# A dense layer's last chunk goes from tiles of 384 tokens to seven products per 2x2 blocks, and expert weight forms are made earlier

## The chip, the cores and the metric

One core of one Trainium2 chip runs the kernel. The metric is device time in microseconds (us) of one execution. Engines: PE (TensorE, matmuls), DVE (VectorE), ACT (ScalarE), SP (SyncE, here only the queue that issues DMAs). PSUM banks hold what TensorE accumulates; VectorE or ScalarE reads it out, here called an eviction.

## The reference

Three layers follow each other on 2304 tokens of width 512: an attention through 32 packed rows per head, a dense layer, and eight experts under a normalised routing matrix. The change touches the dense layer and when the first weights of the experts are prepared.

```python
def _moe_ref(x, w_in, w_out):
    h = x @ w_in                              # 2304x512 @ 512x2048
    g = h * (1.0 / (1.0 + np.exp(-h)))        # silu
    return (g @ w_out).astype(np.float32)     # 2304x2048 @ 2048x512
...
    for e in range(E):                        # 8 experts, after a gate P
        h = np.maximum(x @ w1[e], 0.0)
        out += P[:, e:e + 1] * (h @ w2[e])
```

## The kernel before

Every float32 operand of a product is kept as a rounded high part and a low rest ("hi", "lo"), and each product is three matmuls, hi x hi, hi x lo and lo x hi. Making such a pair is called a split: ScalarE casts the raw tile to hi, then VectorE subtracts hi from the raw tile and writes lo (`split`, L144 to L146). So each split is one ScalarE and one VectorE instruction, and VectorE waits for ScalarE's part.

The dense layer runs in four chunks of 512 hidden columns (`WID`, numbers 0 to 3). In chunks 1 to 3 the loop goes over the four batches of 576 tokens, in chunk 3 in the order 2, 3, 0, 1, and over two halves of 288 tokens each:

- `make_u` (L629) folds the chunk's first weights into the 128 packed attention rows; its 16 matmuls come once per batch and are split into `Uh`, `Ul`.
- `gemm1` (L675) makes the hidden values of a half: 24 matmuls of 288 columns (L652), then per pair of column tiles a silu into `graw` (ScalarE), a cast into `ring` (ScalarE) and the rest into `ring` (VectorE, L685).
- `gemm2_wide` (L723) takes the second matrix for 384 tokens and 128 output columns: 12 matmuls of 384 columns (L736) on a PSUM tile `g2w`. The result is added to the running sum `x2` (tiles `x2a` for batches 0 and 1, `x2b` for 2 and 3), on every other tile by VectorE (L743), on the rest by ScalarE, which puts the sum into PSUM ahead of the matmuls (L721) and copies it out (L741). A chunk has 24 such tiles.

Work for later runs in between. A generator `pre_w1` prepares, for 16 expert weight halves (numbers s = 0 to 15), four sums on VectorE (`sums4`, tiles `S`, L851) and four splits into tiles `po`, which SP stores to DRAM (L841); the raw weights of half s+1 are loaded (`r`, L823) when the sums of half s have been read. Each half takes seven steps of the generator, of which 111 are left when chunk 1 begins. `pump`, called after each pair of column tiles and each wide tile, advances it by `RATE[c]` steps per unit; a chunk has 64 units. Another generator, `convs`, turns the next chunk's 64-bit weights into floats and, for the second matrix, splits them into `woh`, `wol` (L544, L546). In chunk 3 its place is taken by `pre0`, which splits the tokens (`xs`) and the first expert weights (`w1h`, `w1l`, `w2h`, `w2l`) for the stage that follows; that stage begins on TensorE with the gate's matmuls (`lg`, L1235).

The order on TensorE, VectorE and ScalarE is the order in which the code is written. Each engine runs its queue in that order, so an instruction that waits holds up all behind it. PSUM tiles for `g2w` come from a pool of four (`ps3`), those for `gemm1` and `make_u` from a pool of two (`pg`).

Of the kernel before, what the change touches and what calls it, by code (L numbers as in the profile page):

```python
# [9 lines left out]
F32 = mybir.dt.float32  # L10
F32R = mybir.dt.float32r
# [3 lines left out]
ALU = mybir.AluOpType  # L15
# [10 lines left out]
FH = 512  # L26
EPS = 1e-9

RATE = {1: 36 / 64, 2: 36 / 64, 3: 41 / 53}
CONV = 0.6  # L30
TW = 384
LATE = 3
# [73 lines left out]
def fused_kernel(  # L106
# [34 lines left out]
    def unit(shape, dt, name):  # L141
        return wp.tile(shape, dt, tag="w", name=name)
# [98 lines left out]
    win, wout = {}, {}  # L241
# [306 lines left out]

    def convs(c):

        todo = [conv2(c, kind, j) for kind in ("in", "out") for j in range(2)]
        for g in todo[:2]:
            next(g)
        for _ in range(4):
            yield
        for n, g in enumerate(todo):
            for _ in g:
                yield
            if n + 2 < 4:
                next(todo[n + 2])  # L560
            yield
# [797 lines left out]

    with tc.manual_schedule(engines={mybir.EngineType.PE, mybir.EngineType.DVE, mybir.EngineType.Activation}):  # L1360
        for i, (c, b) in enumerate(seq):
            if c == 0:
                continue
            nxt = seq[i + 1] if i + 1 < len(seq) else None

            def pump(w):
                if cvn is not None:
                    if c < NC - 1:
                        pump_conv(w)
                    elif w > 1:  # L1370
                        cvn.step()
                pump_pre(w * RATE[c])

            if b == order[c][0]:
                cvn = Rot([convs(c + 1)], 1) if c + 1 < NC else None
            for half in range(2):
                unit_ = 2 * (b % 2) + half
                if c == NC - 1 and b == order[c][0] and half == 0:
                    cv_st.close()
                if c == NC - 1 and b == order[c][2] and half == 0:  # L1380
                    a2b_st.close()
                    open_("gh", 6)
                    open_("r2", 2)
                    load_w2(0, 0)
                    load_w2(0, 1)
# [4 lines left out]
                if half == 1 and nxt is not None and not first:  # L1390
# [6 lines left out]
                if (c, b) == seq[NC][:2]:  # L1397
                    keep = len(tiles)
                if nxt is None and half == 1:
                    keep = 0  # L1400
                while len(tiles) > keep:
                    n = tiles.pop(0)
                    gemm2_wide(*n, tiles[0] if tiles else None, pump)
                    if n == (NC - 1, order[c][2] // 2, 0, 3):
                        for _ in pre:
                            pass
                        cvn = Rot([pre0()], 1)
        cvn.drain()


    def moe_step(s):
# [150 lines left out]
```

## Time and profile before

| what | value |
|---|---|
| median of 3 runs (lowest, highest) | 1787.64 us (1787.37, 1788.65) |
| profiled execution, its span from first to last instruction | 1785.8 us |
| its own time | not listed beside the span; the median lies 1.84 us above the span |
| TensorE, VectorE, ScalarE busy | 1765.9, 1438.8, 1067.5 us |
| chunk 3, from its first `make_u` to the first `lg` | 279.6 to 373.05 us, 93.45 us |

Times in the rows are us from the span's start. Busy time is a sum of recorded durations; the records of two neighbours on an engine overlap by up to a tenth of a us, so what an instruction really takes in a queue is read from start to start.

### The profile page before, as it was taken

How to read it: one execution, taken by the hardware profiler on the slowest of the kernel's cores; microseconds unless marked ns; L12 is line 12 of the kernel's file. 1: busy time of each engine (PE TensorE's matmuls, PEld its weight loads, DVE VectorE, ACT ScalarE, POOL GpSimd, SP SyncE). 2: the span in 40 equal slices, each digit the busy share in tenths (PEclk: the TensorE clock that was granted, in tenths of full speed). 3: DMA queues.
4: the chain of work that ended last, by engine and by line, in shares of the span. 5: the costliest groups of instructions: out<-in, count | busy, mean ns of one | idle time of the engine just before them, and what ended most of it. 6: DMA issues, size and time to landing. Idle time of an engine off the chain costs nothing.

```text
span 1785.8 us, 25355 instructions
## 1 busy us (share of the span) xinstructions
PE 1765.9 (99%) x9564; PEld 1506.5 (84%) x9564; DVE 1438.8 (81%) x1917; ACT 1067.5 (60%) x1696; POOL 1.0 (0%) x8
## 2 busy tenths in 40 slices
PE   7999999999999999999999999999999999999998
PEld 4999999989998888888888888888888888888887
DVE  7868796758676998999888999887777777777778
ACT  6776676645454666665666665656555555555555
POOL 0000000000000000000000000000000000000000
PEclk9999999999999999999999999999999999999999
DMA  9326676965665655455655545964455544555442
GB/s 348 143 95 214 235 260 246 335 253 180 210 209 172 224 184 177 167 191 192 195 171 175 172 175 199 323 228 165 153 171 161 164 153 144 167 161 168 151 130 94
DMA packets 141498, 341.75 MB, mean 191 GB/s; under 512 B 11952, under 2 KB 49472, under 8 KB 140480
## 3 DMA queue, kind: packets, MB, share of 16 engines
q1 hardware_dynamic: 141376, 340.14, 56.3%
q8 instruction: 75, 1.23, 0.3%
q14 instruction: 47, 0.39, 0.1%
HBM read 256.66 MB, written 83.44 MB: 190 GB/s over the span
## 4 chain that ended last, share of the span: by engine, by line
PE 94%; DVE 2%; DMA 2%; ACT 1%; issue 1%; SPq 0%; DVEq 0%; ACTq 0%
PE d L1153 34%; PE X L1201 19%; PE Z L1201 10%; PE g2w L736 8%; PE g L652 5%; PE Y L1201 5%; PE u L1046 5%; PE d L1065 4%; PE g L704 3%; DMA v<-in_v_dram 1%; PE u L251 1%; DMA kq<-in_kT_dram 0%; PE pp L367 0%; PE s L251 0%; PE lg L1235 0%
## 5 line engine op out<-in xcount | busy, mean ns | idle before, releaser
L146 DVE TENSOR_TENSOR lo<-hb,hi 128x1024 fp32r<-128x1024 f32 x224 | 273.7, 1222 | 33.2 <-ACT hi L145 32.3
L1153 PE MATMUL d<-hi,w2f 128*128 128x512 f32 x896 | 294.2, 389 | 0.0
L1201 PE MATMUL X<-xf,w1l 128*128 128x512 f32 x1152 | 276.9, 389 | 0.0
L145 ACT CAST hi<-hb 128x1024 fp32r<-128x1024 f32 x224 | 235.3, 1052 | 65.2 <-PE d L1153 59.9
L1201 PEld LDWEIGHTS X<-xf,w1l 128*128 128x128 f32 x1152 | 216.2, 188 | 44.9
L1161 ACT COPY M<-d 128x512 f32<-128x512 f32 x234 | 137.3, 588 | 143.2 <-PE d L1153 140.1
L1165 DVE TENSOR_TENSOR M<-d,M 128x512 f32<-128x512 f32 x204 | 140.5, 689 | 101.2 <-PE d L1153 101.2
L1153 PEld LDWEIGHTS d<-hi,w2f 128*128 128x128 f32 x896 | 168.1, 188 | 35.0
L1153 PE MATMUL d<-lo,w2f 128*128 128x512 f32 x448 | 174.3, 389 | 0.0
L1153 PE MATMUL d<-hi,w2l 128*128 128x512 f32 x512 | 167.7, 389 | 0.0
L736 PE MATMUL g2w<-ring,woh 128*128 128x384 f32 x576 | 148.0, 337 | 1.9 <-ACT g2w L721 1.9
L1149 ACT COPY d<-M 128x512 f32<-128x512 f32 x216 | 127.1, 589 | 20.4 <-DVE M L1165 19.0
L1153 PE MATMUL d<-hi,w2g 128*128 128x512 f32 x384 | 125.7, 389 | 0.0
L1153 PEld LDWEIGHTS d<-hi,w2l 128*128 128x128 f32 x512 | 96.1, 188 | 20.3 <-ACT d L1149 0.4
L736 PEld LDWEIGHTS g2w<-ring,woh 128*128 128x128 f32 x576 | 102.7, 188 | 11.6 <-issue 7.5
L1208 ACT COPY cp<-X 128x512 f32<-128x512 f32 x128 | 74.4, 581 | 47.8 <-PE X L1201 47.6
L1153 PE MATMUL d<-lo,w2l 128*128 128x512 f32 x256 | 99.6, 389 | 0.0
L1153 PEld LDWEIGHTS d<-lo,w2f 128*128 128x128 f32 x448 | 84.1, 188 | 17.4
L1201 PE MATMUL Y<-xf,w1f 128*128 128x512 f32 x384 | 97.3, 389 | 0.0
L736 PE MATMUL g2w<-ring,wol 128*128 128x384 f32 x288 | 96.4, 335 | 0.0
L1046 PE MATMUL u<-xs,w1h 128*128 128x256 f32 x512 | 94.4, 285 | 0.0
L145 ACT CAST w1f<-rb 128x512 fp32r<-128x512 f32 x96 | 59.8, 624 | 56.9 <-PE d L1153 41.4
(219 smaller groups left out, 3474.5 us busy)
## 6 DMA issues: line engine op xcount, KB each, us to landing
r<-in_moe_w_dram SPq DMA_DIRECT2D x128, 512.0 KB, 4.1
w1l<-w1d SPq DMA_DIRECT2D x128, 512.0 KB, 4.2
w1d<-po SPq DMA_DIRECT2D x64, 512.0 KB, 4.5
w2d<-w2f SPq DMA_DIRECT2D x64, 512.0 KB, 4.2
w2l<-w2d SPq DMA_DIRECT2D x64, 512.0 KB, 3.6
rb<-in_moe_w_dram SPq DMA_DIRECT2D x96, 256.0 KB, 2.7
sb<-in_moe_w_dram SPq DMA_DIRECT2D x48, 256.0 KB, 2.7
pb<-pd SPq DMA_DIRECT2D x16, 512.0 KB, 5.3
```

What stands on the lines that cost most here:

```text
L145: act.copy(out=hi, in_=raw)
L146: eng.tensor_tensor(out=lo, in0=raw, in1=hi.bitcast(F32), op=ALU.subtract)
L652: pe.matmul(ps, lhs[:, fs], rhs, start=(n == 0), stop=(n == 5))
L736: pe.matmul(ps[:, :TW], lhs[:, f % 2, ds], ring[f // 2][:, 2 * (f % 2) + rhs, q], start=(n == 0 and not on), stop=(n == 11), skip_group_ch ...
L1046: pe.matmul(ps[:, i], w[:, k % 2, f], x[:, k], start=(n == 0), stop=(n == 11))
L1065: pe.matmul(ps, h[:, l, f % 2, 128 * tt:128 * tt + 128], w[:, f % 2], start=(fh == 0 and n == 0), stop=(fh == 1 and n == 11))
L1149: act.copy(out=ps, in_=m)
L1153: pe.matmul(ps, w[:, l, c, 128 * d:128 * d + 128], r[:, c], start=(n == 0 and not seed), stop=(n == 5), skip_group_check=seed)
L1161: act.copy(out=m, in_=ps)
L1165: dve.tensor_tensor(m, ps, m, op=ALU.add)
L1201: pe.matmul(ps, w[:, l, c, 128 * i:128 * i + 128], x[:, r, c], start=(n == 0 and p in (1, 7)), stop=(n == 5), skip_group_check=p in (2, 6, ...
L1208: act.copy(out=t, in_=ps)
```

## The change

Chunks 1 and 2 keep their loop. Their `RATE` goes from 36/64 to 41/64 steps per unit. At the end of chunk 2, `conv2` no longer splits chunk 3's second matrix but leaves the raw floats in `wz`. Chunk 3 is written out by hand. `w_forms` makes seven weight forms `wS` out of the 2x2 blocks of the second matrix. `g_unit` makes hidden values, raw, for one half and two column tiles; `h_form`, `forms_a`, `forms_b`, `forms_c` make the seven token forms `ft` of a batch out of four raw blocks. `product` takes one of seven products with 2 x 6 matmuls of 288 columns on PSUM tiles `sX`, `sZ` or `sY`, all from the pool of four. Four products go into `sX` one after another (1, 6, 5, 3), two into `sZ` (7, 4); after each the state of the PSUM tile is added to an output block by VectorE, and the next product adds on top of it in the same PSUM tile. Product 2 starts from the running sum, put into `sY` by ScalarE. `step` advances `pre_w1` by 0.9 per product or wide tile; after product 2 of the third batch the rest of it is run through at once.

```diff
-RATE = {1: 36 / 64, 2: 36 / 64, 3: 41 / 53}
+RATE = {1: 41 / 64, 2: 41 / 64, 3: 0.9}
...
+            if c == NC - 1:
+                wz[j] = z.rearrange("p (k f) -> p k f", k=2)
+                return
...
+        def step():
+            pump_pre(RATE[c])
+            next(cvn, None)
...
+            form(1, a11)
+            yield
+            dve.tensor_tensor(tb, a11, a21, op=ALU.subtract)
+            form(7, tb)
+            yield
+            dve.tensor_tensor(ta, a21, a22, op=ALU.add)
+            form(5, ta)
...
+        def h_form(k, p, x):
...
+            t = box["ft"][:, fn[0] % 4].rearrange("p (l c s) -> p l c s", l=2, c=2)
+            fn[0] += 1
+            split(t[:, 0], t[:, 1], x)
+            box["f"][k, p] = t
...
+        def forms_b(k):
+            r = box["raw"][k]
+            minus(r[12], r[22], r[12])
+            h_form(k, 7, r[12])
+            minus(r[5], r[22], r[11])
...
+        CH = {1: "X", 6: "X", 5: "X", 3: "X", 7: "Z", 4: "Z", 2: "Y"}
...
+        def product(k, p):
+            w, t, ch = wS[p], box["f"].pop((k, p)), CH[p]
+            for d in range(2):
+                if p in (1, 7):
+                    box[ch, d] = box["p3"].tile([128, 512], F32, tag="y", name=f"s{ch}{k}{d}")
+                ps = box[ch, d][:, :HS]
...
+                if p == 2:
+                    act.copy(out=dst, in_=ps)
+                else:
+                    dve.tensor_tensor(dst, ps, dst, op=ALU.add)
+            step()
...
+        for k in range(4):
...
+            product(k, 1)
+            if more:
+                g_unit(k + 1, 0, 0)
+            h_form(k, 5, r[11])
+            product(k, 7)
+            h_form(k, 2, r[21])
+            product(k, 6)
+            if more:
+                g_unit(k + 1, 0, 1)
+            h_form(k, 3, r[22])
+            product(k, 4)
...
+            product(k, 5)
+            if more:
+                forms_b(k + 1)
+                g_unit(k + 1, 1, 0)
+            product(k, 2)
+            if k == 2:
+                for _ in pre:
+                    pass
+                cvn = pre0()
+            if more:
+                forms_c(k + 1)
+            if k < 2:
+                make_u(c, o[k + 2])
+            product(k, 3)
+            if more:
+                h_form(k + 1, 4, box["raw"][k + 1][5])
```

Three places show how instructions move. The first is VectorE at the head of chunk 3, before: from the first `make_u` of the chunk (`Ul_3387`) on, VectorE has wide tiles' evictions, rests of `ring`, and expert forms.

```order
L638 TENSOR_TENSOR Ul_3387<-u_3377,Uh_3386 128x1024
L743 TENSOR_TENSOR x2b_1372<-g2w_3403,x2b_1372 128x384
L146 TENSOR_TENSOR po_6_3419<-S_2_3333,po_6_3419 128x512
L146 TENSOR_TENSOR po_7_3424<-S_3_3352,po_7_3424 128x512
L685 TENSOR_TENSOR ring_103<-graw,ring_103 128x2x288
L685 TENSOR_TENSOR ring_1745<-graw,ring_1745 128x2x288
```

The same place now, the last 12 of the 34 rows from `Ul_3416` to the eviction of the first product (`sX_3654`); `wsa` is the scratch of `w_forms`, `raw` a raw hidden block, and among the 22 rows ahead of these stand five `wS`, eight expert rows and three evictions.

```order
L641 TENSOR_TENSOR Ul_3621<-u_3611,Uh_3620 128x1024
L1460 TENSOR_TENSOR raw_3468<-raw_3470,raw_3468 128x576
L146 TENSOR_TENSOR ft<-raw_3468,ft 128x576
L1460 TENSOR_TENSOR raw_3471<-raw_3470,raw_3467 128x576
L1427 TENSOR_TENSOR wsa<-ct_3045,wsa 128x512
L146 TENSOR_TENSOR wS_3629<-wsa,wS_3629 128x512
L146 TENSOR_TENSOR ft<-raw_3471,ft 128x576
L1460 TENSOR_TENSOR raw_3471<-raw_3469,raw_3471 128x576
L146 TENSOR_TENSOR wS_3649<-ct_3045,wS_3649 128x512
L146 TENSOR_TENSOR ft<-raw_3471,ft 128x576
L1509 TENSOR_TENSOR x2b_1369<-sX_3654,x2b_1369 128x288
L1509 TENSOR_TENSOR x2b_1370<-sX_3662,x2b_1370 128x288
```

All weight forms and the first four token forms now stand in VectorE's queue ahead of the first product's eviction.

The second place is VectorE near the end of chunk 3, before: the expert forms of the last half (s = 15: `S_1_4149` to `po_3_4205`) stand around a wide tile's eviction, and the tokens' splits (`xs`) follow.

```order
L851 TENSOR_TENSOR S_4_4168<-r_151_4048,S_2_4151 128x512
L743 TENSOR_TENSOR x2a_790<-g2w_4174,x2a_790 128x384
L146 TENSOR_TENSOR po_6_4190<-S_2_4151,po_6_4190 128x512
L146 TENSOR_TENSOR po_7_4195<-S_3_4166,po_7_4195 128x512
L146 TENSOR_TENSOR po_5_4200<-S_1_4149,po_5_4200 128x512
L146 TENSOR_TENSOR po_3_4205<-S_4_4168,po_3_4205 128x512
L146 TENSOR_TENSOR xs_4224<-x2b_1369,xs_4223 128x128
```

Now, after product 2 of the third batch: eight rows of half 14 (`S_1_4295` to `po_3_4322`, not shown) and these of half 15 stand in one piece, ahead of a token form, a subtraction, and the eviction of the third batch's product 3 (`sX_4114`, `sX_4122`).

```order
L854 TENSOR_TENSOR S_1_4327<-r_150_4303,r_151_4305 128x512
L854 TENSOR_TENSOR S_2_4329<-S_1_4327,r_150_4303 128x512
L854 TENSOR_TENSOR S_3_4331<-r_150_4303 128x512
L854 TENSOR_TENSOR S_4_4333<-r_151_4305,S_2_4329 128x512
L146 TENSOR_TENSOR po_6_4339<-S_2_4329,po_6_4339 128x512
L146 TENSOR_TENSOR po_7_4344<-S_3_4331,po_7_4344 128x512
L146 TENSOR_TENSOR po_5_4349<-S_1_4327,po_5_4349 128x512
L146 TENSOR_TENSOR po_3_4354<-S_4_4333,po_3_4354 128x512
L146 TENSOR_TENSOR ft<-rawt,ft 128x576
L1460 TENSOR_TENSOR rawt<-rawt 128x576
L1509 TENSOR_TENSOR x2a_787<-sX_4114,x2a_787 128x288
L1509 TENSOR_TENSOR x2a_788<-sX_4122,x2a_788 128x288
```

Sixteen expert rows that were spread over the chunk, with evictions between them, now follow one another.

The third place is TensorE beside it, now: products 2 and 3 of the third batch (`sY_4240`, `sX_4114`), then 1, 7 and 6 of the fourth (`sX_4384`, `sZ_4406`, `sX_4384` again). Before, wide tiles stood here.

```order
L1501 MATMUL sY_4240<-ft,wS_3649 128x288 x6
L1501 MATMUL sY_4242<-ft,wS_3649 128x288 x6
L1501 MATMUL sX_4114<-ft,wS_3629 128x288 x6
L1501 MATMUL sX_4122<-ft,wS_3629 128x288 x6
L1501 MATMUL sX_4384<-ft,wS_3488 128x288 x6
L1501 MATMUL sX_4392<-ft,wS_3488 128x288 x6
L1501 MATMUL sZ_4406<-ft,wS_3509 128x288 x6
L1501 MATMUL sZ_4414<-ft,wS_3509 128x288 x6
L1501 MATMUL sX_4384<-ft,wS_3568 128x288 x6
L1501 MATMUL sX_4392<-ft,wS_3568 128x288 x6
```

In the fourth batch no hidden values are left to make, so the products follow each other with nothing between them.

## Rows read from the trace of the kernel before

**Rows 1.** The page, busy time of each engine.

```profile
PE 1765.9 (99%) x9564; PEld 1506.5 (84%) x9564; DVE 1438.8 (81%) x1917; ACT 1067.5 (60%) x1696; POOL 1.0 (0%) x8
```

**Rows 2.** Waits, those of PE: waited for, us in total, times, longest.

```profile
PE g2w L736 <- ACT g2w L721: 1.9, 2, 1.6
```

**Rows 3.** Windows: stretch, PE, PEld, DVE, ACT, POOL busy, PEclk, DMA share, GB/s.

```profile
10.00:15.00 5.00, 4.47 (x37) 2.06 (x38) 3.53 (x7) 1.86 (x4) 0.00 (x0) 1.00 1.02 418
...
133.00:213.00 80.00, 78.20 (x526) 74.64 (x525) 64.00 (x92) 53.23 (x84) 0.00 (x0) 1.00 0.70 243
213.00:279.60 66.60, 66.28 (x443) 62.55 (x441) 54.73 (x78) 46.58 (x75) 0.00 (x0) 1.00 0.62 230
...
279.60:373.05 93.45, 93.45 (x617) 88.71 (x616) 63.41 (x101) 58.51 (x107) 0.00 (x0) 1.00 0.77 282
```

**Rows 4.** Timeline of PE: start, duration, instructions, idle before and releaser.

```profile
179.21 0.62 PE L736 MATMUL g2w<-ring,woh 128*128 128x384 f32 x2 [1.63 <-ACT g2w L721]
...
284.91 0.29 PE L652 MATMUL g<-a2h,Uh 128*128 128x288 f32 x1
...
288.10 0.51 PE L736 MATMUL g2w<-ring,woh 128*128 128x384 f32 x2
...
292.26 0.29 PE L652 MATMUL g<-a2h,Uh 128*128 128x288 f32 x1
...
295.54 1.09 PE L251 MATMUL u<-win,ppT 64*32 64x512 f32 x16
296.56 0.62 PE L736 MATMUL g2w<-ring,woh 128*128 128x384 f32 x2
...
373.05 2.17 PE L1235 MATMUL lg<-x2b,wg 128*32 128x256 f32 x26
```

**Rows 5.** Timeline of DVE in chunk 3.

```profile
282.04 1.22 DVE L638 TENSOR_TENSOR Ul<-u,Uh 128x1024 fp32r<-128x1024 f32 x1
...
350.38 0.76 DVE L685 TENSOR_TENSOR ring<-graw,ring 128x576 fp32r<-128x576 f32 x1 [0.85 <-ACT ring L684]
351.06 0.69 DVE L851 TENSOR_TENSOR S<-r,r 128x512 f32<-128x512 f32 x1
351.78 0.69 DVE L851 TENSOR_TENSOR S<-S,r 128x512 f32<-128x512 f32 x1
...
353.59 0.55 DVE L743 TENSOR_TENSOR x2a<-g2w,x2a 128x384 f32<-128x384 f32 x1
354.06 2.49 DVE L146 TENSOR_TENSOR po<-S,po 128x512 fp32r<-128x512 f32 x4
356.46 0.29 DVE L146 TENSOR_TENSOR xs<-x2b,xs 128x128 fp32r<-128x128 f32 x1
356.66 0.29 DVE L146 TENSOR_TENSOR xs<-x2a,xs 128x128 fp32r<-128x128 f32 x1
...
374.20 1.22 DVE L146 TENSOR_TENSOR w2l<-r,w2h 128x1024 fp32r<-128x1024 f32 x1
375.33 0.41 DVE L1239 COPY lgs<-lg 96x256 f32<-96x256 f32 x1
```

**Rows 6.** Groups of instructions by line, ACT from 279.6 to 373.05.

```profile
L145 ACT CAST po<-S 128x512 fp32r<-128x512 f32 x28 | 16.5, 621 | 1.4 <-DVE S L851 1.4
L684 ACT CAST ring<-graw 128x576 fp32r<-128x576 f32 x17 | 11.5, 674 | 0.5
L683 ACT ACTIVATE graw<-g 128x576 f32<-128x576 f32 x17 | 11.1, 650 | 16.5 <-PE g L652 16.5
```

**Rows 7.** DMA issues from 279 to 376: count, KB each, median us to landing.

```profile
r<-in_moe_w_dram SPq DMA_DIRECT2D x20, 512.0 KB, 4.9
```

**Rows 8.** Timeline of PE in the span's first 20 us.

```profile
10.19 1.18 PE L251 MATMUL s<-kq,pTs 64*32 64x288 f32 x8 [10.19 <-DMA kq<-in_kT_dram]
11.71 2.15 PE L251 MATMUL s<-kq,pTs 64*32 64x288 f32 x24 [0.34 <-DMA kq<-in_kT_dram]
...
18.00 1.20 PE L251 MATMUL s<-kq,pTs 64*32 64x288 f32 x32
```

More of the change, by code (lines that the diff above doesn't have):

```diff
@@ L240, in fused_kernel @@
     kqn = []
-    win, wout = {}, {}
+    win, wout, wz = {}, {}, {}
     NC = len(WID)
@@ L1361, in fused_kernel @@
         for i, (c, b) in enumerate(seq):
-            if c == 0:
+            if c in (0, NC - 1):
                 continue
-            nxt = seq[i + 1] if i + 1 < len(seq) else None
+            nxt = seq[i + 1]
             def pump(w):
[L1367 to L1371, printed above, removed]
+                pump_conv(w)
                 pump_pre(w * RATE[c])
             if b == order[c][0]:
-                cvn = Rot([convs(c + 1)], 1) if c + 1 < NC else None
+                cvn = Rot([convs(c + 1)], 1)
             for half in range(2):
                 unit_ = 2 * (b % 2) + half
[L1378 to L1385, printed above, removed]
                 first = (c, b) == seq[NC][:2]
@@ L1389, in fused_kernel @@
                 gemm1(c, b, half, pump)
-                if half == 1 and nxt is not None and not first:
+                if half == 1 and not first:
                     if nxt[0] != c:
@@ L1396, in fused_kernel @@
                 keep = {0: 2, 1: 2, 2: 2, 3: 4}[unit_]
-                if (c, b) == seq[NC][:2]:
+                if first:
                     keep = len(tiles)
-                if nxt is None and half == 1:
-                    keep = 0
                 while len(tiles) > keep:
@@ L1403, in fused_kernel @@
                     gemm2_wide(*n, tiles[0] if tiles else None, pump)
[L1404 to L1408, printed above, removed]
+        cv_st.close()
+        c, o = NC - 1, order[NC - 1]
+        cvn = iter(())
+        hr, hr_st = pool("hr", 1, side="right", reuse_waits="tile")
+        wS, box["raw"], box["f"] = {}, {}, {}
+        fn = [0]
+        def step():
+            pump_pre(RATE[c])
+            next(cvn, None)
@@ new lines, in w_forms, with form @@
+        def w_forms():
+            a11, a21 = wz[0][:, :, 0:256], wz[0][:, :, 256:512]
+            a12, a22 = wz[1][:, :, 0:256], wz[1][:, :, 256:512]
+            ta, tb = (hr.tile([128, 2, 256], F32, tag=f"w{n}", name=f"ws{n}") for n in "ab")
+            def form(p, x):
+                wS[p] = unit([128, 2, 2, 256], F32R, f"wS{p}")
+                split(wS[p][:, 0], wS[p][:, 1], x)
+            form(1, a11)
[5 more added lines that the diff above has]
+            form(5, ta)
+            yield
+            dve.tensor_tensor(ta, ta, a11, op=ALU.subtract)
+            form(6, ta)
+            yield
+            form(4, a22)
+            yield
+            dve.tensor_tensor(ta, a12, ta, op=ALU.subtract)
+            form(3, ta)
+            yield
+            form(2, a12)
+            yield
@@ new lines, in raw_set, with g_unit @@
+        def raw_set(k):
+            if k == 0:
+                return [hr.tile([128, 2, HS], F32, tag=f"r{n}", name=f"raw{n}") for n in range(5)]
+            if k == 1:
+                box["rt"] = hp.tile([128, 8, 2, HS], F32, tag="h1", name="rawt")
+            if k == 2:
+                return [box["rt"][:, n] for n in (5, 6, 7)] + \
+                    [gt.tile([128, 2, HS], F32, tag="graw", name=f"raw2{n}") for n in range(2)]
+            return [box["rt"][:, n] for n in range(5)]
+        def g_unit(k, j, half):
+            if k not in box["raw"]:
+                box["raw"][k] = dict(zip((11, 12, 21, 22, 5), raw_set(k)))
+            ps = box["pg"].tile([128, 2, 512], F32, tag="pg", name=f"g1_{k}{half}{j}")
+            for i in range(2):
+                gemm1_mm(ps[:, i, :HS], c, o[k], half, 2 * j + i)
+            act.activation(box["raw"][k][10 * (j + 1) + half + 1], ps[:, :, :HS], AF.Silu)
@@ new lines, in h_form, with minus, forms_a @@
+        def h_form(k, p, x):
+            if "ft" not in box:
+                box["ft"] = hp.tile([128, 4, 2 * S], F32R, tag="h0", name="ft")
+            t = box["ft"][:, fn[0] % 4].rearrange("p (l c s) -> p l c s", l=2, c=2)
+            fn[0] += 1
+            split(t[:, 0], t[:, 1], x)
+            box["f"][k, p] = t
+        def minus(out_, a, b_):
+            dve.tensor_tensor(out_, a, b_, op=ALU.subtract)
+        def forms_a(k):
+            r = box["raw"][k]
+            h_form(k, 1, r[11])
+            minus(r[11], r[12], r[11])
@@ new lines, in forms_b, with forms_c, acc_of @@
+        def forms_b(k):
+            r = box["raw"][k]
+            minus(r[12], r[22], r[12])
+            h_form(k, 7, r[12])
+            minus(r[5], r[22], r[11])
+        def forms_c(k):
+            r = box["raw"][k]
+            h_form(k, 6, r[5])
+            minus(r[5], r[21], r[5])
+        CH = {1: "X", 6: "X", 5: "X", 3: "X", 7: "Z", 4: "Z", 2: "Y"}
+        OUT = {1: (0, 0), 6: (1, 0), 5: (1, 1), 3: (0, 1), 7: (1, 1), 4: (1, 0), 2: (0, 0)}
+        def acc_of(k, p, d):
+            dh, half = OUT[p]
+            b = o[k]
+            off = (b % 2) * S + half * HS
+            return x2[b // 2][2 * dh + d][:, off:off + HS]
@@ new lines, in seed2 @@
+        def seed2(k):
+            for d in range(2):
+                box["Y", d] = box["p3"].tile([128, 512], F32, tag="y", name=f"sY{k}{d}")
+                act.copy(out=box["Y", d][:, :HS], in_=acc_of(k, 2, d))
+        def product(k, p):
+            w, t, ch = wS[p], box["f"].pop((k, p)), CH[p]
+            for d in range(2):
+                if p in (1, 7):
+                    box[ch, d] = box["p3"].tile([128, 512], F32, tag="y", name=f"s{ch}{k}{d}")
+                ps = box[ch, d][:, :HS]
+                n = 0
+                for f in range(2):
+                    for l, r in ((0, 0), (0, 1), (1, 0)):
+                        pe.matmul(ps, w[:, l, f, 128 * d:128 * d + 128], t[:, r, f],
+                                  start=(n == 0 and p in (1, 7)), stop=(n == 5),
+                                  skip_group_check=p not in (1, 7))
+                        n += 1
+                dst = acc_of(k, p, d)
+                if p == 2:
[3 more added lines that the diff above has]
+            step()
@@ new lines, in wide @@
+        def wide():
+            n = tiles.pop(0)
+            gemm2_wide(*n, tiles[0] if tiles else None, lambda w: step())
+        wf_ = w_forms()
+        g_unit(0, 0, 0)
+        next(wf_)
+        wide()
+        next(wf_)
+        g_unit(0, 0, 1)
+        wide()
+        next(wf_)
+        wide()
+        next(wf_)
+        wide()
+        forms_a(0)
+        g_unit(0, 1, 1)
+        next(wf_)
+        make_u(c, o[1])
+        forms_b(0)
+        next(wf_)
+        g_unit(0, 1, 0)
+        forms_c(0)
@@ new lines, in fused_kernel @@
+        next(wf_)
+        h_form(0, 4, box["raw"][0][5])
+        for k in range(4):
+            r, more = box["raw"][k], k < 3
+            if k == 1:
+                hr_st.close()
+                a2b_st.close()
+                open_("gh", 6)
+                open_("r2", 2)
+                load_w2(0, 0)
+                load_w2(0, 1)
+            product(k, 1)
[10 more added lines that the diff above has]
+            if more:
+                forms_a(k + 1)
+                g_unit(k + 1, 1, 1)
+            seed2(k)
+            product(k, 5)
[3 more added lines that the diff above has]
+            product(k, 2)
+            if k == 2:
+                for _ in pre:
[6 more added lines that the diff above has]
+            product(k, 3)
+            if more:
+                h_form(k + 1, 4, box["raw"][k + 1][5])
@@ L1411, in moe_step @@
+        for _ in cvn:
+            pass
     def moe_step(s):
```

## The prediction

> **What bounds the kernel now.** I read the page's busy times first. TensorE is busy 99% of the span, VectorE 81%, ScalarE 60% [rows 1]. The list of waits then says how much of TensorE's time is lost: past the start, whose idle time is in [rows 8], the longest wait is one of 1.6 us [rows 2]. So the kernel is bound by TensorE's queue, and a change pays what it takes out of that queue, as long as no other engine falls behind. The windows give the cushion by stage. In chunk 3, from its first `make_u` at 279.60 to the first `lg` at 373.05, TensorE is busy 93.45 of 93.45 us and VectorE 63.41 [rows 3]. In chunk 1 (133 to 213) VectorE has 64.0 of 80.0, in chunk 2 54.7 of 66.6 [rows 3].
>
> **TensorE's part.** From 284.91 to 288.10 stand 24 matmuls of 288 columns, 133 ns each; from 288.10 to 292.26 two wide tiles, 24 matmuls of 384 columns, 173 ns each [rows 4]. The change removes 24 wide tiles of 2.08 us, 49.9 us, and adds 4 x 7 products of 12 matmuls, 28 x 1.60 = 44.7 us. Hidden values, `make_u` and the six wide tiles left from chunk 2 stay. If TensorE never waits, the stage takes 93.45 - 49.9 + 44.7 = 88.2 us: 5.2 us less.
>
> **VectorE's part.** Costs are read from start to start where VectorE doesn't wait [rows 5]: 128x512 0.60 us (four from 354.06 to 356.46), 128x576 0.68 (350.38 to 351.06), 0.12 more where a row reads the one before (351.06 to 351.78), eviction of 384 columns 0.47 (353.59 to 354.06), 128x1024 1.13 (374.20 to 375.33), 128x128 0.20 (356.46 to 356.66). An eviction of 288 columns isn't there; it lies between 0.20 and 0.47, and on the line through both it is 0.37, which I take.
>
> The order of the changed kernel gives VectorE, from the chunk's first `Ul` to the last product's eviction: 54 rows of 512 columns (23 `po` and 20 `S` of the experts, 7 `wS` and 4 sums for them), 44 of 576 (28 `ft`, 16 subtractions), 48 evictions of 288 and 3 of 384, 7 of 1024, 8 `xs`. That is 32.4 + 29.9 + 17.8 + 1.4 + 7.9 + 1.6 = 91.0 us. VectorE's queue becomes longer than TensorE's 88.2, before any wait. The seven-product form saves a product and pays with 12 additions per batch and twelve evictions; the move of expert forms takes away only about ten rows, since 43 are left. (At 0.20 or 0.47 per eviction the sum is 82.8 or 95.8.)
>
> So where VectorE waits decides. Four places, with zero at the first `make_u`:
>
> 1. *Head of the chunk.* TensorE has six wide tiles (12.5), four pairs of hidden tiles (6.4) and two `make_u` (1.0 each by [rows 4], with a gap 2.2) ahead of product 1, which ends at 22.8; with the next pair and product 7, product 6 could start at 26.0. It accumulates in the PSUM tile of product 1 and must wait until VectorE has read that out. That eviction has 34 rows from `Ul` on. `Ul` starts at 2.4 (282.04 [rows 5]), the rows cost 21.2, which would be in time, at 23.6. But the 11th row evicts a wide tile that TensorE ends at 12.7, and the 24 rows from there cost 14.8: 27.7. On top, five splits follow directly on the row that makes their raw tile, so VectorE stands while ScalarE casts, 0.62 to 0.67 us each [rows 6], once with a silu of 0.65 ahead: 3.5 us. Product 6 starts near 31.4. TensorE loses 5.4 us; 1.7 if the casts were all hidden.
> 2. *The first three batches.* Per batch TensorE has 11 x 1.60 + 1.2 = 18.8, VectorE 12 x 0.37 + 11 x 0.68 + 1.13 + some seven expert rows, 17.3, one cast wait of 0.7, and about 0.4 for rows that read the row before. Nearly even: VectorE never catches up. I take 0.4 per batch, 1.2; at best nothing.
> 3. *The rest of the expert forms in one piece.* 111 steps are due; chunks 1 and 2 take 2 x 64 x 41/64 = 82, and the 24 calls of `step` up to product 2 of the third batch 21. So two halves, 16 rows, run at once, and behind them stands the eviction of the third batch's product 3. Call E the end of product 2 on TensorE. VectorE is then 1.2 behind (eviction of 5, subtraction, cast, `ft`, subtraction). The first half takes 4.9. The second needs raw weights whose load may start only when the first half's four sums have read the buffer, 2.5 in, and such a load lands 4.9 after issue [rows 7]: 7.4. Then 4.9 more, `ft`, subtraction and eviction 1.9: E + 15.4. TensorE has products 3 and 1 meanwhile, 3.2, for the last batch has no hidden tiles left to fill in. Product 7 needs a PSUM tile of the pool of four: two hold the new `sX`, the other two are the old `sX` that wait for that eviction. TensorE stands 12.2 us; 9.7 if the load is there in time.
> 4. *The last batch.* VectorE still has 12 evictions, five `ft`, `xs` and the 1024-wide splits of the next stage between products of 1.60. I put 1.9 on it, 0 at best.
>
> Sum: 88.2 + 5.4 + 1.2 + 12.2 + 1.9 = 108.9 against 93.45, +15.5 us. Cross-check on VectorE: start 2.4, work 91.0, waits 7.5 at the head, 2.1 for casts in the batches, 2.5 for the load, 2.4 for rows that depend on the row before: 107.9.
>
> *Chunks 1 and 2.* Five more steps each, 5.7 rows of 0.60 = 3.4 us of VectorE; chunk 2 sheds two splits (2 x 1.13). There is room in the mean, but one wait shows how a full VectorE reaches TensorE there: 1.63 us at 179.21 [rows 4]. Bounds 0 and 4.5 (all of it on the path); by the wait that exists I take 0.5.
>
> *DMAs.* The same stores and loads, none added. Where they come earlier, DMA share goes up in chunks with 0.62 and 0.70, and down in one with 0.77 [rows 3].
>
> Together 1785.8 + 15.5 + 0.5 = 1801.8 for the span; the median lies 1.84 above the span of the profiled run: **1803.6, say 1803.5**.
>
> **A rule against the change, weighed.** TensorE stands still for 10.19 us at the start, and afterwards 24 small matmuls take 2.15 us, 90 ns each, where 32 of the same shape take 1.20, 38 ns each, at 18.00 [rows 8]; the granted clock is 1.00 there, the level of 2.4 GHz [rows 3]. Some of it can be the second load, so the rows allow a slow restart, not prove one. The Trainium skill (TensorE: Matmul & The Clock Gate, Part 1) says that TensorE falls to 1.2 GHz when idle and comes back only after work; by that the products after a 12 us stall run at half rate. The granted clock at the start doesn't show such a fall.
>
> **Rivals.**
>
> - *The saving arrives.* 1787.64 - 5.2 = 1782.4, faster. One mechanism: VectorE keeps ahead of every reuse of a PSUM tile. It speaks for it that VectorE has 30 us free in the stage now [rows 3]. It decides from the point where VectorE's queue, waits included, is under 88 us and the 16 rows run ahead of the third batch's evictions. Against it: 91.0 us without waits, and the position in the order.
> - *VectorE packs better.* ScalarE runs ahead so that casts cost nothing, the load is in time: stalls 1.7 + 0 + 9.7 + 0, stage 99.6, time 1793.8; with evictions at the cheap bound some us less, down to about 1788.
> - *A slower restart.* After the stall of place 3 the next 12 to 24 matmuls take 266 instead of 133 ns: 1.6 to 3.2 us more, 1805 to 1807, still in the range; together with evictions at 0.47 (48 x 0.10 = 4.8) 1810 to 1812.
> - *Not much is moved.* If the moved forms cost chunks 1 and 2 their upper bound: 4 us more, 1807.5.
>
> **How the numbers follow.** The forecast, VectorE as the bound with one long stall, gets 0.78, slower restart and upper bound of the moved forms within it. Better packing gets 0.10 (0.04 of it inside 0.2%), the saving 0.06, worse than 1809 0.06. Within 0.2% (3.6 us, about what a measurement of this kernel can tell from no change) means 1784.1 to 1791.2. Faster 0.06, same 0.04, slower 0.90. The range takes the lower end between the sums with and without the waits' upper values, and the upper end with either dear evictions or a slow restart: 1796 to 1809.
>
> **What the changed profile would show.** Chunk 3's products start to start at 1.60 us where none waits (the 88.2). A wait of product 6 in the first batch of 4 to 6 us, released by VectorE. A wait of product 7 in the fourth batch of 9 to 13 us, released by the eviction of `sX`, while VectorE runs 16 rows `S` and `po`, with a gap in the middle for the DMA of `r`. VectorE busy above 90% of the stage. An eviction of 288 columns at about 0.45 recorded, 0.37 start to start. What would make it wrong: evictions much cheaper, expert forms already done by then, or a product that waits for none of this because the PSUM pool gives it another tile.

## The result, and the profile after

The changed kernel takes 1810.03 us, the median of 4 runs (1807.97 to 1810.79), against 1787.72 before: 1.0121 times as long, with a 95% interval of 1.0107 to 1.0135. The direction was right, and both forecast stalls stand where they were put, but the time is 6.5 us above the forecast and 1.0 above its range. The profiled run is the fastest of the four: 1807.97 us, span 1806.2.

The page's busy times, to compare with [rows 1]: TensorE now stands 42 us of its span (20 before), and VectorE has 35 us more to do.

```profile
PE 1764.3 (98%) x9612; PEld 1504.6 (83%) x9612; DVE 1473.7 (82%) x1990; ACT 1070.2 (59%) x1705; POOL 1.0 (0%) x8
```

The list of TensorE's waits answers to [rows 2] (waited for: us in total, times, longest):

```profile
PE sZ L1501 <- DVE x2a L1509: 13.8, 1, 13.8
...
PE sX L1501 <- DVE x2b L1509: 4.8, 1, 4.8
PE g2w L739 <- ACT g2w L724: 4.1, 3, 2.2
PE g L655 <- DVE Ul L641: 1.7, 3, 1.0
```

The windows, columns as in [rows 3]: first the stretch from the `make_u` at 127.82 to the first `make_u` of chunk 3 (below: "chunks 1 and 2"; 150.36 us before, from 129.24 to 279.60), then chunk 3 from there to the first `lg`:

```profile
127.82:281.37 153.55, 148.74 (x1002) 140.07 (x1001) 123.93 (x180) 102.26 (x165) 0.00 (x0) 1.00 0.71 253
...
281.37:393.44 112.07, 92.22 (x665) 87.03 (x665) 93.74 (x165) 60.72 (x114) 0.00 (x0) 0.91 0.53 193
```

Chunks 1 and 2 became 3.2 us longer and chunk 3 18.6. What lies ahead of 127.82 is 1.4 shorter, which came and went from kernel to kernel (the same `make_u` starts at 127.8 to 129.8 in all that follow, where the code up to there is nearly the same); from the first `lg` on nothing changed (1412.8 us in both).

TensorE's timeline in chunk 3, as in [rows 4]. The products are `sX`, `sY`, `sZ`, 12 matmuls each (24: two products):

```profile
302.75 1.76 PE L1501 MATMUL sX<-ft,wS 128*128 128x288 f32 x12
306.57 1.72 PE L1501 MATMUL sZ<-ft,wS 128*128 128x288 f32 x11 [0.18 <-DVE ft L146]
313.14 3.22 PE L1501 MATMUL sX<-ft,wS 128*128 128x288 f32 x12 [4.85 <-DVE x2b L1509]
...
332.00 0.40 PE L655 MATMUL g<-a2h,Ul 128*128 128x288 f32 x1 [0.97 <-DVE Ul L641]
...
365.10 3.36 PE L1501 MATMUL sX<-ft,wS 128*128 128x288 f32 x24
382.24 3.25 PE L1501 MATMUL sZ<-ft,wS 128*128 128x288 f32 x12 [13.77 <-DVE x2a L1509]
385.28 1.83 PE L1501 MATMUL sX<-ft,wS 128*128 128x288 f32 x12
386.95 1.76 PE L1501 MATMUL sZ<-ft,wS 128*128 128x288 f32 x12
...
391.75 1.76 PE L1501 MATMUL sX<-ft,wS 128*128 128x288 f32 x12
393.44 2.11 PE L1238 MATMUL lg<-x2b,wg 128*32 128x256 f32 x25
```

At 313.14 product 6 of the first batch had waited 4.85 us for the eviction of product 1; at 382.24 product 7 of the last batch had waited 13.77. Both products then take 3.0 us to the next instruction's start, instead of 1.60. The windows of TensorE (busy, granted clock, DMA share, GB/s) say why: the clock is at 0.50 there, 1.2 GHz, and is full again from 318 and from 386 on.

```profile
312.00:316.00 4.00, 2.86 (x12) 0.50 0.31 124
316.00:318.00 2.00, 2.00 (x13) 0.71 0.04 14
318.00:320.00 2.00, 2.00 (x17) 1.00 0.66 262
372.00:384.00 12.00, 1.76 (x7) 0.50 0.96 352
384.00:386.00 2.00, 2.00 (x12) 0.65 1.04 419
386.00:388.00 2.00, 2.00 (x17) 1.00 0.66 268
```

VectorE's timeline ahead of product 7 shows the forecast block: four sums, four rests, a gap for the load, the same again, then `ft`, a subtraction and at last the eviction.

```profile
366.27 0.69 DVE L854 TENSOR_TENSOR S<-r,r 128x512 f32<-128x512 f32 x1
...
368.80 2.49 DVE L146 TENSOR_TENSOR po<-S,po 128x512 fp32r<-128x512 f32 x4
374.71 0.69 DVE L854 TENSOR_TENSOR S<-r,r 128x512 f32<-128x512 f32 x1 [3.42 <-DMA r<-in_moe_w_dram]
...
379.06 1.29 DVE L146 TENSOR_TENSOR po<-S,po 128x512 fp32r<-128x512 f32 x2 [0.52 <-ACT po L145]
380.27 0.75 DVE L146 TENSOR_TENSOR ft<-rawt,ft 128x576 fp32r<-128x576 f32 x1
381.06 0.76 DVE L1460 TENSOR_TENSOR rawt<-rawt 128x576 f32<-128x576 f32 x1
381.73 0.81 DVE L1509 TENSOR_TENSOR x2a<-sX,x2a 128x288 f32<-128x288 f32 x2
```

### The profile page after: what moved, and what is told of

The parts are those of the page before. It is cut to its first block, busy times and chain, and to the rows that moved or that the text cites. A ratio compares the mean times of both kernels' runs of the same rounds, so it can differ in the third digit from the quotient of the medians.

```text
span 1806.2 us, 25552 instructions
## 1 busy us (share of the span) xinstructions
PE 1764.3 (98%) x9612; PEld 1504.6 (83%) x9612; DVE 1473.7 (82%) x1990; ACT 1070.2 (59%) x1705; POOL 1.0 (0%) x8
## 4 chain that ended last, share of the span: by engine, by line
PE 90%; DVE 5%; DMA 2%; ACT 2%; issue 1%; SPq 0%; DVEq 0%; ACTq 0%
PE d L1156 33%; PE X L1204 19%; PE Z L1204 10%; PE Y L1204 5%; PE u L1049 5%; PE d L1068 4%; PE g L655 4%; PE g2w L739 4%; PE g L707 3%; DMA v<-in_v_dram 1%; DMA w1d<-po 1%; DVE S L854 1%; PE sX L1501 1%; PE sZ L1501 0%; DVE po L146 0%
## 5 line engine op out<-in xcount | busy, mean ns | idle before, releaser
L739 PE MATMUL g2w<-ring,woh 128*128 128x384 f32 x384 | 98.8, 338 | 4.1 <-ACT g2w L724 4.1
L1204 PE MATMUL Z<-xf,w1l 128*128 128x512 f32 x384 | 92.2, 389 | 0.0
L1204 PE MATMUL X<-xf,w1f 128*128 128x512 f32 x384 | 92.2, 389 | 0.0
```

The costliest lines, as they stand in the source:

```text
L739: pe.matmul(ps[:, :TW], lhs[:, f % 2, ds], ring[f // 2][:, 2 * (f % 2) + rhs, q], start=(n == 0 and not on), stop=(n == 11), skip_group_ch ...
L1204: pe.matmul(ps, w[:, l, c, 128 * i:128 * i + 128], x[:, r, c], start=(n == 0 and p in (1, 7)), stop=(n == 5), skip_group_check=p in (2, 6, ...
```

## The experiments

The theory: VectorE's queue bounds chunk 3, and its two lumps (layer's forms at the head, 16 expert rows before the last batch) stall TensorE. Its rivals: the seven products are no cheaper in themselves; the move alone is the loss; the fallen clock is the loss. All times below are medians of 4 runs (10 for the move alone) beside runs of the kernel before (1787.0 to 1787.5) on the same chip; the two chunk columns are from the profiled run, by the same marks as above, and the waits are those of product 6 (first batch) and product 7 (last batch).

| kernel | time, us | ratio, 95% interval | chunks 1, 2 | chunk 3 | p6 waits | p7 waits |
|---|---|---|---|---|---|---|
| before | 1787.72 | 1 | 150.36 | 93.45 | - | - |
| after | 1810.03 | 1.0107 to 1.0135 | 153.55 | 112.07 | 4.85 | 13.77 |
| the move alone | 1790.61 | 1.0010 to 1.0029 | 153.53 | 93.07 | - | - |
| no block | 1803.10 | 1.0073 to 1.0103 | 155.10 | 105.64 | 4.85 | 1.20 |
| no block, no move | 1805.74 | 1.0087 to 1.0120 | 150.33 | 110.86 | 4.85 | 1.52 |
| more moved | 1800.88 | 1.0060 to 1.0090 | 158.54 | 98.92 | 4.86 | 0.77 |
| all moved | 1820.80 | 1.0173 to 1.0203 | 181.62 | 95.96 | 4.58 | none |
| 72 idle matmuls before p7 | 1811.34 | 1.0118 to 1.0152 | 153.55 | 112.82 | 4.85 | filled |
| 60 idle matmuls before p7 | 1810.18 | 1.0110 to 1.0141 | 155.09 | 112.00 | 4.85 | filled |
| 20 idle matmuls before p6 | 1810.39 | 1.0112 to 1.0146 | 155.13 | 111.29 | filled | 13.71 |
| two forms later | 1811.53 | 1.0119 to 1.0153 | 153.55 | 112.03 | 3.19 | 13.62 |
| two forms later, no block | 1805.52 | 1.0086 to 1.0116 | 153.55 | 107.62 | 3.19 | 1.21 |
| sums, rests on GpSimd | 1812.25 | 1.0120 to 1.0154 | 155.13 | 113.59 | 4.85 | 14.72 |
| and the layer's forms | 1815.79 | 1.0144 to 1.0174 | 150.36 | 122.04 | 4.69 | 12.1 |

**The move alone.** The kernel before, with only the rates of chunks 1 and 2 changed.

```diff
-RATE = {1: 36 / 64, 2: 36 / 64, 3: 41 / 53}
+RATE = {1: 41 / 64, 2: 41 / 64, 3: 41 / 53}
```

> The kernel before with only the rates of chunks 1 and 2 at 41/64 (chunk 3's 41/53 and its wide tiles stay). Theory: the earlier forms are what moved the start of chunk 3 by 1.8 us; chunk 3 then starts near 281.4 and the time is 1788.5 to 1790. Rival (the 1.8 us comes from elsewhere, such as another order of loads): no change, 1787.7, chunk 3 starts at 279.6.

It costs 3.1 us (the time lies 0.6 above the theory's range), all of it in chunks 1 and 2, and these show the same waits there as the changed kernel: 2.23, 0.52 and 1.31 us for a PSUM tile `g2w`, where before had 1.63 and 0.31. So this term, which the prediction put at 0.5, is 3.2, and it belongs to the move. ScalarE's queue shows how rows reach TensorE although VectorE has room. First ScalarE before, at the wait of 1.63:

```profile
177.21 1.04 ACT L544 CAST woh<-ct 128x1024 fp32r<-128x1024 f32 x1 [1.20 <-DVE ct L539]
...
178.68 0.47 ACT L721 COPY g2w<-x2b 128x384 f32<-128x384 f32 x1
```

Then ScalarE and TensorE in the move alone:

```profile
178.23 1.05 ACT L544 CAST woh<-ct 128x1024 fp32r<-128x1024 f32 x1 [1.80 <-DVE ct L539]
...
179.70 0.47 ACT L721 COPY g2w<-x2b 128x384 f32<-128x384 f32 x1
...
180.22 0.61 PE L736 MATMUL g2w<-ring,woh 128*128 128x384 f32 x2 [2.23 <-ACT g2w L721]
```

Two more `po` rows now stand on VectorE among the steps that make `ct`. ScalarE waits 0.60 us longer for `ct`, and the copy that puts the running sum into TensorE's PSUM tile stands behind that cast. At the third wait (0.31 before, 1.31 now) two more casts of `po`, 0.52 each, stand on ScalarE ahead of that copy.

**No block, no block without the move, more moved, all moved.** The changed kernel with four other tables of rates, in this order. The expert rows left in chunk 3 are 43 (as in the changed kernel, but spread evenly), 52, 28 and 0.

```diff
-RATE = {1: 41 / 64, 2: 41 / 64, 3: 0.9}
+RATE = {1: 41 / 64, 2: 41 / 64, 3: 1.5}
...
+RATE = {1: 36 / 64, 2: 36 / 64, 3: 1.9}
...
+RATE = {1: 48 / 64, 2: 48 / 64, 3: 0.9}
...
+RATE = {1: 62 / 64, 2: 62 / 64, 3: 0.9}
```

> The 16 expert rows stay in chunk 3 but run at 1.5 steps per product, so that none is left in one piece after product 2 of the third batch. Theory 1 (VectorE's queue is the bound of the chunk, 91 us of rows plus its waits): the 13.8 us wait of product 7 in the last batch goes, but the rows now delay the evictions of the first three batches; what is gained is the 3.4 us wait for the load, the slow restart of 1.4 us and some of the rest, chunk 3 takes 103 to 108 us instead of 112.1, the time is 1801 to 1806. Rival (only the place of the rows counts, VectorE has room elsewhere in the chunk): all of 13.8 + 1.4 comes back, chunk 3 takes 97, the time is 1795.

> The seven products without the move: chunks 1 and 2 at the rate of before (36/64), so that 52 expert rows are left in the last chunk instead of 43, and there the rate of 1.9, with which no block of them is left. To be compared with the kernel of rate 1.5, which has the move and no block either (chunk 3 105.64, 1803.1 us). Theory 1 (VectorE's queue bounds chunk 3, and the move saves there about what it costs earlier): chunk 3 takes 109 to 111.5 us, chunks 1 and 2 fall from 155.1 to about 150.4, and the time is 1802 to 1805. Rival (the move is a plain loss): chunk 3 takes less than 107 us and the time is under 1800.

> Chunks 1 and 2 run 48/64 steps per unit instead of 41/64, chunk 3 as in the change (0.9), so that no expert row is left in one piece and 16 rows fewer stand in chunk 3. Theory 1 (length of VectorE's queue in chunk 3): the queue is 81 instead of 91 us, TensorE's own 88 bounds again after the head; chunk 3 takes 95 to 98 us. What chunks 1 and 2 lose is the open part: by the mean room of VectorE nothing, by the 1.8 us that the move of five steps cost some 2 to 4 us more; time 1794 to 1799. Rival (chunks 1 and 2 are as full as chunk 3): they lose as much as chunk 3 gains and the time stays near 1808.

> The changed kernel with the rates of chunks 1 and 2 at 62/64, so that all expert forms are made there and none of the 43 rows is left in chunk 3. Theory 1 (expert rows on VectorE cause both stalls of chunk 3, and TensorE's saving is there behind them): VectorE's queue is 91 - 43 x 0.60 = 65 us against TensorE's 88.2; the wait of product 6 in the first batch is 0 to 2 us instead of 4.9, there is none of product 7, and chunk 3 takes 89 to 92 us instead of 112, against 93.45 before the change. The 26 us of VectorE rows go to chunks 1 and 2, which take 12 to 25 us more than the changed kernel's 153.6, so the total stays between 1797 and 1812. Rival (the seven products with their additions are too slow for VectorE by themselves): chunk 3 takes 95 or more with waits of 3 us or more at the head.

With the same 43 rows spread evenly the 13.8 us wait is gone and chunk 3 is 6.4 us shorter, not 13: waits of 1.4 us for `Ul` and others come up in its place. Without the move chunk 3 is 5.2 longer and chunks 1 and 2 are 4.8 shorter, but 1.55 of these 4.8 is a fall of the clock in the profiled run of "no block", which other runs of the same code lack (last section). By the medians the kernel with the move is 2.6 us faster, so here the move pays for itself. Between 52 and 43 rows chunk 3 changes by 5.22 us, 0.58 per row, a row's full price on VectorE; between 43 and 28 by 0.45 per row; between 28 and 0 by 0.11. So with some 40 rows VectorE bounds the chunk, and below 28 it hardly depends on them. That bears the theory out, though not all of its ranges. With 43 rows spread evenly they held. Without the move the time came out 0.7 us above, and with more moved chunk 3 0.9 and the time 1.9 above. With all moved the time came out 8.8 above, and the 89 to 92 us for chunk 3 did not come (the rival's 95 or more did), and that is the most telling run. Its window and TensorE's wait:

```profile
311.43:407.39 95.96, 91.02 (x665) 85.88 (x664) 68.16 (x122) 49.55 (x91) 0.00 (x0) 0.96 0.18 65
```

```profile
PE sX L1501 <- DVE x2b L1509: 4.6, 1, 4.6
```

VectorE has 28 us to spare, and the chunk still takes 2.5 us more than before the change: 88.2 for TensorE, 4.6 for the wait at the head, 2.1 for the matmuls at half clock behind it (1.9 in the changed kernel) and 1.4 for the last batch, where VectorE sets the pace (below), are 96.3, 0.4 more than measured. Ahead of the awaited eviction, from the wide tile's eviction at 324.29 on, VectorE stands 3.9 us for ScalarE's casts. So the seven products save 5.2 us of TensorE's time by the prediction's sum, and their own forms and evictions cost some 7.8. The forms moved away cost 28 us in chunks 1 and 2 (forecast 12 to 25), more than the 26 they take on VectorE.

**Two forms later.** The weight forms of products 3 and 2 stand behind products 6 and 4, at the rate of the change and at 1.5.

```diff
         forms_b(0)
-        next(wf_)
         g_unit(0, 1, 0)
         forms_c(0)
-        next(wf_)
...
             product(k, 6)
+            if k == 0:
+                next(wf_)
...
             product(k, 4)
+            if k == 0:
+                next(wf_)
```

> The changed kernel with the weight forms of products 3 and 2 made behind products 6 and 4 of the first batch instead of ahead of product 1. Theory 1 (the wait at the head comes from the layer's own forms that stand ahead of the first eviction on VectorE, not from the expert rows): 3 rows of 0.60 and a wait of 0.69 for a cast, some 2.5 us, leave the stretch ahead of the eviction, product 6 waits about 2.4 us instead of 4.85, and with the clock not fallen, or less, the third make_u comes 2.5 to 4 us earlier against the chunk's first one. The later wait of 13.8 us stays. The time is 2 to 4 us less than that of the changed kernel if VectorE lets it through. Rival (the rows only move behind, and VectorE has no room for them): the wait at the head is shorter, but the third make_u comes less than 1 us earlier.

> The same new place of the two weight forms, and in the last chunk the rate of 1.5, with which no block of expert rows is left before product 7 of the last batch. Theory 1 (VectorE's queue bounds this chunk, so what is saved at the head comes back as other waits once the block is gone): chunk 3 takes 102 to 105 us against 105.64 with the rate alone, time 1800 to 1803, still slower than before by over 0.6%. Rival (head and block are the only losses): chunk 3 takes 97 or less, time 1795 or less.

The wait at the head fell by 1.66, not 2.5: with fewer rows between a cast and its rest, two rests of `ft` waited 0.74 us each for ScalarE, where they had waited 0.41 and nothing. And what was gained is lost again: the third `make_u` comes 0.78 us earlier (44.14 after the first instead of 44.92), the last product 7 0.34, the first `lg` 0.04. The first kernel's rival was right. Without the block the chunk even takes 2 us more than with the forms in their old place (107.62 against 105.64). That chunk and the time (1805.52) lie above the theory's ranges, and far from the rival's 97 and 1795.

**Idle matmuls in the stalls.** They keep TensorE at work where it would stand, 72 and then 60 of them ahead of product 7 in the last batch, 20 ahead of product 6 in the first. Nothing reads their output.

```diff
+            if k == 3:
+                ps = box["pg"].tile([128, 2, 512], F32, tag="pg", name="keep")
+                for _ in range(60):
+                    pe.matmul(ps[:, 0, :128], ident, ident, start=True, stop=True)
```

> The change, with 72 idle matmuls of 128 columns on a free PSUM tile between products 1 and 7 of the last batch, so that TensorE does not stand still in the long wait. Nothing else changes. Theory (granted clock falls in the wait, and costs 1.4 us behind it): product 7 takes 1.6 instead of 3.0 us, the mean granted clock rises, the time falls by about 1.4 us to 1808.6. Rival (product 7 is slow because of something else, such as its operands or VectorE beside it): product 7 still takes 3.0 us and the time stays at 1810.

> The changed kernel with 60 idle matmuls (no output of theirs is read) between product 1 and product 7 of the last batch, where TensorE otherwise stands 13.8 us. 72 of them took 16.2 us, so 60 should take about 13.5 and end just with the wait. Theory 1 (the clock falls in the stall and the products behind it run at half rate): product 7 takes 1.6 to 1.7 us instead of 3.04, the granted clock stays at 1.0 around 382, and the time is 1 to 1.6 us less than that of the changed kernel, about 1808.5. Rival (the long product 7 waits for evictions, not for the clock): it takes 3 us here too, time unchanged.

> The changed kernel with 20 idle matmuls (nothing reads them) in front of product 6 of the first batch, where TensorE otherwise stands 4.85 us; they should take 4.5. Theory 1 (a fallen clock costs time where TensorE, not VectorE, paces the batch): product 6 takes 1.6 to 1.9 us instead of 3.04 with the granted clock at 1.0, and the third make_u of the chunk comes 1 to 1.9 us earlier against the chunk's first one. Rival (VectorE paces here too, as in the last batch, where the kept clock gave product 7 back 1.2 us and the end of the chunk only 0.2): product 6 is as short, but waits for VectorE come up behind it and the next make_u comes less than 0.5 us earlier. The time of the whole moves by at most 2 us either way, too little for the runs to tell.

72 took 16.2 us, over two more than the wait; product 7 then takes 1.68 us, as the theory has it, but the time did not fall (1811.34 against a forecast of 1808.6). With 60 the fit is right. TensorE's timeline (each idle matmul stands as two records):

```profile
371.07 13.56 PE L1553 MATMUL keep<-ident 128*128 128x128 f32 x120
384.85 1.85 PE L1501 MATMUL sZ<-ft,wS 128*128 128x288 f32 x12 [0.21 <-DVE x2a L1509]
386.74 1.82 PE L1501 MATMUL sX<-ft,wS 128*128 128x288 f32 x12
388.54 1.83 PE L1501 MATMUL sZ<-ft,wS 128*128 128x288 f32 x12
...
395.88 0.85 PE L1238 MATMUL lg<-x2b,wg 128*32 128x256 f32 x9
```

The granted clock is 1.00 throughout, and product 7 takes 1.89 us to the next one's start instead of 3.04. The clock was the cause of the long product. But the time is no less, which neither theory nor rival had together with a short product 7: from product 7 to `lg` are 11.03 us, against 11.20 in the changed kernel. VectorE's timeline in the same run says why:

```profile
384.34 0.81 DVE L1509 TENSOR_TENSOR x2a<-sX,x2a 128x288 f32<-128x288 f32 x2
...
386.14 0.82 DVE L1509 TENSOR_TENSOR x2a<-sX,x2a 128x288 f32<-128x288 f32 x2
...
387.94 0.82 DVE L1509 TENSOR_TENSOR x2a<-sZ,x2a 128x288 f32<-128x288 f32 x2
```

It evicts a product every 1.80 us, with `xs`, `xs` and `ft` between, without a gap, and TensorE's products take that pace. In the changed kernel VectorE goes at the same 1.80, but product 7 at half clock gives it a lead, and the products behind it follow at 1.60 to 1.69 without a wait. The two losses lie over each other, and only one is paid. At the head it is otherwise:

```profile
311.75 4.73 PE L1555 MATMUL keep<-ident 128*128 128x128 f32 x40 [0.75 <-ACT raw L1449]
316.24 1.84 PE L1501 MATMUL sX<-ft,wS 128*128 128x288 f32 x12
...
327.60 1.09 PE L251 MATMUL u<-win,ppT 64*32 64x512 f32 x16
```

Product 6 is short, the third `make_u` comes 43.52 us after the first (44.92 in the changed kernel), and the last product 7 is still 1.47 earlier. So the clock costs 1.4 us on the path at the first stall, and 0.2 at the second. (In this run it stayed at 0.50 until 388 behind the second stall, and from product 7 to `lg` are 11.89 us: where it comes back later, it outlasts VectorE's pace.)

**On GpSimd.** Sums `S` and rests of the expert forms in chunk 3 on GpSimd; in the second kernel the layer's forms too, with rates 36/64, 36/64 and 1.6.

```diff
-        dve.tensor_tensor(t, a, b, op=op)
+        box.get("eng", dve).tensor_tensor(t, a, b, op=op)
...
-        split(t[:, 0], t[:, 1], x)
+        split(t[:, 0], t[:, 1], x, box.get("eng", dve))
...
+        box["eng"] = nc.gpsimd
```

> The changed kernel with the sums S and the rests of the expert weight forms that are left in chunk 3 on GpSimd; VectorE keeps the evictions, ft and the weight forms of the layer itself. Theory 1 (VectorE's queue with the 16 rows in it is what holds product 7 back): the 13.8 us wait is gone or below 4, the wait of product 6 in the first batch falls to 3.5 or less as some rows in front of its eviction leave VectorE, chunk 3 takes 93 to 98 us instead of 112, time 1790 to 1796. Rival (GpSimd is slow enough, or disturbs VectorE enough, that the forms come late): chunk 3 stays above 105, with waits of TensorE or VectorE for GpSimd, or the next stage starts late.

> As the kernel with sums and rests of the expert forms on GpSimd, and the forms of the layer's own weights there too (sums and rests), with chunks 1 and 2 taking their expert forms at the rate of before, so that more of them fall into chunk 3, on GpSimd. Theory 1 (TensorE's saving is real and only VectorE's queue eats it): no wait of product 6 above 2 us, chunk 3 takes 89 to 92 us against 93.45 before, chunks 1 and 2 take 150 to 151, time 1782 to 1787, faster than before. Rival (GpSimd's rows are late): products wait for their weight forms or the expert stage for its own, chunk 3 above 95, time 1790 or more.

Both rivals held. Groups of instructions in chunk 3, first kernel (count, busy us, mean ns, idle before and releaser):

```profile
L146 DVE TENSOR_TENSOR ft<-rawt,ft 128x576 fp32r<-128x576 f32 x18 | 17.8, 991 | 16.4 <-ACT ft L145 16.3
L1461 DVE TENSOR_TENSOR rawt<-rawt 128x576 f32<-128x576 f32 x9 | 12.1, 1348 | 0.2
...
L1510 DVE TENSOR_TENSOR x2b<-sX,x2b 128x288 f32<-128x288 f32 x16 | 6.5, 446 | 0.0
```

```profile
L146 POOL TENSOR_TENSOR po<-S,po 128x512 fp32r<-128x512 f32 x20 | 29.4, 1482 | 37.7 <-ACT po L145 37.7
```

A rest takes 1.48 us on GpSimd (0.68 on VectorE), and VectorE's own subtractions take 1.35 us in the mean instead of 0.76, up to 1.85 where GpSimd is at work beside them. The block is as long as before, and ScalarE hands it on in the order of its queue, seen here in ScalarE's and then VectorE's timeline:

```profile
378.79 0.62 ACT L145 CAST po<-S 128x512 fp32r<-128x512 f32 x1 [6.94 <-POOL S L854]
```

```profile
382.46 1.80 DVE L146 TENSOR_TENSOR ft<-rawt,ft 128x576 fp32r<-128x576 f32 x1 [11.05 <-ACT ft L145]
```

The cast for the next `ft` stands behind casts that wait for GpSimd's sums, so the eviction behind that `ft` waits as it did behind the rows themselves.

## Why the prediction was right, and where it failed

- **TensorE's 88.2 us**: right. Products follow at 1.60 us where none waits, and 88.2 with the measured losses gives the chunk's time in the kernel without expert rows to 0.4.
- **Place 1**: forecast 5.4, measured 4.85 and 0.18. The price is right, though the prediction's own terms add up to less than it wrote (12.7 + 14.8 is 27.5, with 3.5 for the casts 31.0, so 5.0); the casts measured 3.2. But of the rows ahead of the eviction the layer's own forms and the casts in order carry it; without any expert row 4.58 remain.
- **Place 2**: forecast 1.2, measured 0.97.
- **Place 3**: forecast 12.2, measured 13.77. The load came 3.42 us late instead of 2.5, one more cast wait took 0.52. The 16 rows were read off the order; the tally of steps beside them (82 and 21 of 111) leaves 8, little more than one half. Chunk 1 takes 20 wide tiles, not 24, and so has some 55 units instead of 64; with that about 13 steps are left, nearly two halves.
- **Place 4**: forecast 1.9, measured 1.60. VectorE's pace is 1.80 us a product, as supposed, but in the changed kernel the loss stands in product 7 at half clock (3.05); VectorE's pace takes 1.4 only where the clock is kept. That the two come out alike is luck.
- **The clock**: a failed step. The prediction left it out of the sum and looked for it behind the long stall only. It fell at both, costs 0.2 behind the long one, where VectorE sets the pace anyway, and 1.9 at the head: 1.41 in product 6 and 0.45 in the matmuls behind it, 1.4 of it shown by the idle matmuls. The Trainium skill (TensorE: Matmul & The Clock Gate, Part 1) has TensorE fall to 1.2 GHz when idle; the trace agrees, with 0.50 granted. Whether TensorE paces the work behind the stall decided the price.
- **Chunks 1 and 2**: the other failed step, and the larger one. "By the wait that exists I take 0.5" was wrong; 3.2 in the profiled run, 4.7 where the clock falls as well (last section). The prediction counted VectorE's rows alone; the wait at a full VectorE grew by 0.6, and another grew by 1.0 through the casts of the same forms on ScalarE (the move alone). The bound of 4.5, and the rival built on it, were the better guide.
- **A sign that failed**: VectorE was to be busy above 90% of the stage. It is busy 93.74 of 112.07 us, 84%, and the prediction's own 91.0 of 108.9 is 84% as well. VectorE bounds the chunk by its order and its waits, not by being busy throughout.

The terms sum up: 2.7 too little for chunks 1 and 2, 1.9 for the clock at the head and 1.6 at place 3, 0.9 too much at places 1, 2 and 4, and 0.6 of chunk 3 that no wait accounts for, make 5.9; the shorter start takes 1.4 back, which with rounding gives the profiled run's 1807.97. The median lies 2.06 above that run. What the other three runs had more isn't profiled; the last section has a possible cause.

## What to carry to other kernels

A form that takes work from the bounding engine is priced with the chain that feeds it: here 5.2 us of TensorE's time were bought with rows on VectorE that cost more even when VectorE was 71% busy, mostly because they and their casts stand one behind the other ahead of the first eviction. Work spread over an engine with room in the mean is not free; the rows moved to chunks 1 and 2 cost about 0.3 us of time for each 0.6 us row, and more than 0.6 when all were moved. Count a moved form on every engine that it uses, and look what stands behind it in each queue. A stall's clock loss counts only where the stalled engine also sets the pace behind it, so look who paces there before adding or leaving it out.

## What was unexpected in the hardware

The same wait of 2.23 us for `g2w` near 179 stands in eight of the profiled kernels that share the code of chunks 1 and 2 with the changed one. In four of them (the changed kernel among them) the granted clock stays at 1.00 behind it and chunks 1 and 2 take 153.55 us; in the other four it falls, and they take 155.09 to 155.13. TensorE's windows of the kernel without the block, one of these:

```profile
178.00:180.00 2.00, 0.87 (x5) 1.00 1.05 324
180.00:182.00 2.00, 2.00 (x10) 0.64 0.99 276
182.00:184.00 2.00, 2.00 (x8) 0.51 0.85 328
184.00:186.00 2.00, 2.00 (x15) 1.00 0.96 307
```

So one and the same wait costs 1.55 us more or not, by something that the code does not fix; the rows don't say what. It could be part of what the changed kernel's other three runs have over its fastest (1.64 to 2.82 us), but that isn't shown: those runs have no trace, and in the kernel "two forms later, no block" a profiled run without the fall lies only 0.4 to 0.7 us below the others.

GpSimd at work makes VectorE's rows with two operands in SBUF longer (0.76 to 1.35 us in the mean, up to 1.85), while evictions, whose one operand comes from PSUM, stay at 0.45. The Trainium skill (SBUF — State Buffer, Who interferes with whom) says that a VectorE instruction with two SBUF inputs contends with a GpSimd instruction that reads SBUF, and one with at most one such input, outside VectorE's 2-port modes, doesn't; the rows agree.
